# Three tiles of the first up product summed during the opening, and the second batch moved around the end of the weight conversion

## The chip, the core and the metric

The kernel runs on one core of a Trainium2 chip. The metric is device time in microseconds (us) of one execution. Five engines work side by side, each in its own order of instructions: PE (TensorE, matmuls; PEld is its weight loads), DVE (VectorE), ACT (ScalarE), POOL (GpSimd) and SP (SyncE, which here issues nearly all DMAs). [...]

## The reference

The inputs are `q`, `k`, `v` of shape 8 batches x 8 heads x 576 positions x 64, all float32, `g_norm` of 64, and the weights `w_in` (512 x 2048) and `w_out` (2048 x 512), which arrive as 64-bit floats and have to be turned into float32 on the chip.

```python
kv  = np.einsum('bhsd,bhse->bhde', k, v)
out = np.einsum('bhsd,bhde->bhse', q, kv)
rms = np.sqrt(np.mean(out * out, axis=-1, keepdims=True) + 1e-06)
x   = (out / rms * g_norm)            # then (B,H,S,D) -> (B*S, H*D): 4608 x 512
h   = x @ w_in
g   = np.maximum(h, 0.0) ** 2
y   = g @ w_out                       # 4608 x 512
```

## The kernel before

The 4608 tokens are cut into nine strips of 512 (`s` = 0 to 8). Each strip has an "up" part (times `w_in`), a squared ReLU and a "down" part (times `w_out`). From strip 1 on the products are seven block products in place of eight (`p` = 1 to 7, order `ORDER = (1, 2, 6, 5, 7, 3, 4)`), which need sums of blocks, made on DVE. Strip 0 is computed while the weights are still being converted, so its up part is the plain product: 16 tiles of `d_ff`, each four matmuls of 128x512 (`up_first`, L609), one per pair of heads. The 16 tiles use PSUM banks by the tag `"ABAC"[2 * fh + i]`: A has two buffers, B and C one each. So tile 5 needs the bank of tile 1, tile 6 that of tile 2, and so on. ACT empties a tile (ReLU L616 and square L617, twice each).

**The conversion.** 32 pieces of 512 KB come from DRAM (SP, L193) into eight `raw` buffers. For each, ACT does two instructions (L205 into a tile `w_c`, of which there are four, and L208), then DVE four (L217, L219, L223, L226). Pieces are converted in pairs; pieces 0 to 15 are `w_in`, 16 to 31 are `w_out`, and the last four pairs (`sums_out`) also take eight subtractions (L243) and four DMAs of the block sums `wt` to the DRAM tensor `w_out` (L276). `convert(n)` emits the pairs below `n`, with ACT's two instructions running one pair ahead. In the loop over the 16 up tiles the conversion is emitted ahead of the tile:

```python
if s == 0 and i < n_up:
    convert(5 + (3 * i + 2) // 4)
    ...
fn(*a)
```

**The opening.** Batch 0 is taken pair of heads by pair of heads (`p` = 0 to 3): `transposed_query` T (PE transposes L334, copied by ACT), `key_value` K (L352, copied by ACT L354, L355), `first_queries` Q (L433), `first_normalized` N (DVE, to L440), `first_features` F (PE transposes L457, copied by ACT L458 into `xT`). Between them lie the first four pieces. Their order is a list written out by hand, `slices`, of which `attend(n)` emits all up to number `n`. Every engine executes in the order in which its instructions are emitted.

**The second batch.** Its eight T and K slices are emitted after up tiles 8 to 15 (T, K, T, K, ...); T and K share two PSUM banks (tag `at`), so a slice needs the copy of the slice two before it. Its queries (L383), norms and features follow in the first six steps of strip 0's down part. Its loads (L120, L128) and those of the rest rows (L143, L151) are issued at up steps 2 and 4 and by K itself.

**Down, strips 0 and 1.** `down(s, p, i)` is one half of a block product (L573, 16 matmul rows of 128x256 per half, 32 per `p`). Its weights are `w_in`'s spare room for `p` = 1, 2, 5 of strip 0, and else a tile `w_blk` loaded from DRAM by `stream()` (L657). Strip 1 also makes the weights for the later, deeper strips: `deep_sums` (DVE, L243, four per `p`) fills a tile `w_t`, which is written to the DRAM tensor `w_deep` (L696). `w_blk` and `w_t` share four buffers. Two DMAs in flight never share one of eight completion counters, so each DMA also waits for the one eight before it.

## Time and profile before

| | us |
|---|---|
| median of 8 runs | 943.46 |
| lowest, highest | 941.71, 945.88 |
| the profiled execution | 944.16 |
| its span on the core | 942.4 |
| around the span | 1.76 |
| PE busy / DVE busy / ACT busy | 917.2 / 658.1 / 227.0 |
| first matmul of strip 0's up part | 31.0 |
| first matmul of strip 0's down part | 95.8 |
| strip 1: first up and first down matmul | 149.9, 207.8 |
| strip 2: first up matmul | 259.2 |

Times in views of the trace are us from the start of the span. A row of a timeline has start, duration, engine, line, operation, output and input, and the number of instructions merged into it; in square brackets stands the idle time in front of it, and what ended it. One fp32 matmul shows as two matmul rows, so "x8" for L609 is one tile of four matmuls.

### The profile page before, as it was taken

Reading aid. Unit: us, or ns where it says so; the run is one execution under the profiler, and the core shown is the slowest. Engines: PE = TensorE matmul, PEld = TensorE weight load, DVE = VectorE, ACT = ScalarE, POOL = GpSimd, SP = SyncE. Lnnn points to the kernel's source line nnn. Section 1 sums busy time; section 2 is a strip of 40 time slices with the busy share of each in tenths; the row PEclk is TensorE's granted clock in tenths of the full one; section 3 lists DMA queues with packets and bytes.
Section 4 is the critical chain, followed back from the end, with each engine's and each line's share of the span. In section 5 each row is a group of like instructions: output and inputs, shape, how many; then the busy total and the mean of one; then the engine's idle time right before and its main releaser. Section 6 shows DMA issues by size and latency. Waiting matters only on the chain.

```text
span 942.4 us, 17026 instructions
## 1 busy us (share of the span) xinstructions
PE 917.2 (97%) x6880; PEld 806.1 (86%) x6880; DVE 658.1 (70%) x1147; ACT 227.0 (24%) x494; POOL 1.7 (0%) x7
## 2 busy tenths in 40 slices
PE   5899999999899999999999999999999999999998
PEld 4444887888788998899989998899889988998898
DVE  4999845585436996489737975697559854983496
ACT  4797332320023102210222013200320022002200
POOL 0000000000000000000000000000000000000000
PEclk9899999999999999999999999999999999999999
DMA  9799782637875586648664874477516831681075
GB/s 276 247 280 313 261 243 107 138 109 251 286 242 138 177 299 195 148 154 290 212 155 113 312 245 126 111 282 254 165 40 236 298 102 57 224 304 65 1 260 177
DMA packets 164286, 185.94 MB, mean 197 GB/s; under 512 B 83952, under 2 KB 137712, under 8 KB 155632
## 3 DMA queue, kind: packets, MB, share of 16 engines
q1 hardware_dynamic: 163888, 184.72, 61.2%
q8 instruction: 54, 0.88, 0.4%
q10 hardware_dynamic: 320, 0.13, 0.1%
q14 instruction: 24, 0.20, 0.1%
HBM read 153.62 MB, written 31.20 MB: 196 GB/s over the span
## 4 chain that ended last, share of the span: by engine, by line
PE 90%; DMA 4%; DVE 3%; ACT 1%; issue 1%; SPq 0%; DVEq 0%; ACTq 0%
PE ps_A L573 30%; PE ps_B L758 18%; PE ps_B L573 14%; PE ps_A L758 14%; PE ps_C L573 7%; PE kv_ps L352 2%; PE x_ps L383 2%; PE ps_A L609 2%; DMA raw<-in_moe_w_out_dram 1%; DMA k_rest<-in_k_dram 1%; DMA w_blk<-w_out 1%; PE ps_B L609 1%; DVE w_c L223 1%; DMA raw<-in_moe_w_in_dram 1%; PE ps_C L609 0%
## 5 line engine op out<-in xcount | busy, mean ns | idle before, releaser
L573 PE MATMUL ps_A<-x_t,w_in 128*128 128x256 f32 x768 | 183.2, 381 | 0.0
L573 PEld LDWEIGHTS ps_A<-x_t,w_in 128*128 128x128 f32 x768 | 144.4, 190 | 20.3 <-ACT snap L583 0.3
L758 PE MATMUL ps_B<-w_blk,g_s 128*128 128x128 f32 x896 | 109.2, 275 | 0.0
L758 PEld LDWEIGHTS ps_B<-w_blk,g_s 128*128 128x128 f32 x896 | 104.6, 192 | 0.0
L758 PE MATMUL ps_B<-w_blk,gt 128*128 128x128 f32 x672 | 84.2, 275 | 0.0
L758 PE MATMUL ps_A<-w_blk,g_s 128*128 128x128 f32 x672 | 81.9, 275 | 0.0
L758 PEld LDWEIGHTS ps_B<-w_blk,gt 128*128 128x128 f32 x672 | 80.1, 192 | 0.4
L758 PEld LDWEIGHTS ps_A<-w_blk,g_s 128*128 128x128 f32 x672 | 78.4, 192 | 0.0
L632 DVE TENSOR_TENSOR gt<-ps_A,snap 128x512 f32<-128x512 f32 x32 | 22.1, 691 | 73.9 <-PE ps_A L573 73.9
L583 ACT COPY snap<-ps_A 128x512 f32<-128x512 f32 x68 | 39.8, 586 | 135.7 <-PE ps_A L573 126.9
L633 DVE SCALAR_TENSOR_TENSOR gt<-gt 128x512 f32<-128x512 f32 x96 | 66.4, 692 | 3.3
L632 DVE TENSOR_TENSOR gt<-ps_C,snap 128x512 f32<-128x512 f32 x32 | 22.1, 690 | 63.4 <-PE ps_C L573 63.4
L758 PE MATMUL ps_A<-w_blk,gt 128*128 128x128 f32 x504 | 63.1, 275 | 0.0
L573 PE MATMUL ps_A<-xT,w_in 128*128 128x256 f32 x256 | 61.3, 382 | 0.0
L573 PE MATMUL ps_C<-xT,w_in 128*128 128x256 f32 x256 | 61.1, 381 | 0.0
L573 PE MATMUL ps_B<-xT,w_in 128*128 128x256 f32 x256 | 61.0, 381 | 0.0
L573 PE MATMUL ps_B<-x_t,w_in 128*128 128x256 f32 x256 | 61.0, 381 | 0.0
L243 DVE TENSOR_TENSOR gt<-gt 128x2048 f32<-128x2048 f32 (+1 forms) x31 | 58.1, 1873 | 4.0 <-PE ps_C L573 3.8
L758 PEld LDWEIGHTS ps_A<-w_blk,gt 128*128 128x128 f32 x504 | 59.7, 192 | 0.0
L573 PEld LDWEIGHTS ps_B<-xT,w_in 128*128 128x128 f32 x256 | 48.2, 190 | 6.7
L573 PEld LDWEIGHTS ps_B<-x_t,w_in 128*128 128x128 f32 x256 | 48.2, 190 | 6.7
L573 PEld LDWEIGHTS ps_C<-xT,w_in 128*128 128x128 f32 x256 | 48.1, 190 | 6.7
(116 smaller groups left out, 1171.7 us busy)
## 6 DMA issues: line engine op xcount, KB each, us to landing
w_blk<-w_deep SPq DMA_DIRECT2D x49, 1024.0 KB, 5.2
w_blk<-w_out SPq DMA_DIRECT2D x49, 768.0 KB, 5.1
w_blk<-w_out SPq DMA_DIRECT2D x11, 1024.0 KB, 6.9
raw<-in_moe_w_in_dram SPq DMA_DIRECT2D x16, 512.0 KB, 5.6
raw<-in_moe_w_out_dram SPq DMA_DIRECT2D x16, 512.0 KB, 5.6
k<-in_k_dram SPq DMA_DIRECT2D x30, 256.0 KB, 2.9
v<-in_v_dram SPq DMA_DIRECT2D x30, 256.0 KB, 3.2
w_deep<-w_t SPq DMA_DIRECT2D x7, 1024.0 KB, 8.5
```

Of the source, the lines that this page charges most:

```text
L223: yield nc.vector.scalar_tensor_tensor(out=ci, in0=high, scalar=-(2**30), in1=ci, op0=ALU.bitwise_and, op1=ALU.bitwise_or)
L243: eng.tensor_tensor(out=out, in0=a, in1=b, op=ALU.subtract)
L352: nc.tensor.matmul(ps[ts(h, D)], lhsT=a, rhs=w, start=c == 0, stop=c == C)
L383: nc.tensor.matmul(ps[half, r, i, ts(p, D)], lhsT=q[row, half], rhs=kvd[b, p][row, row], start=True, stop=True)
L573: nc.tensor.matmul(bank[BANK[p]][:, i, :], lhsT=lhsT(k), rhs=rhs(k), start=p in (1, 5, 2) and i == 0 and k == 0, stop=k == n - 1, skip_gro ...
L583: nc.scalar.copy(snap[p], b)
L609: nc.tensor.matmul(ps, lhsT=w_in[:, kc % KH, g, kc // KH * 2 + fh, ts(i, P)], rhs=xt[0][:, :, kc, :], start=kc == 0, stop=kc == NP - 1,)
L632: nc.vector.tensor_tensor(out=o, in0=b, in1=a, op=ALU.add)
L633: nc.vector.scalar_tensor_tensor(out=o, in0=o, scalar=0.0, in1=o, op0=ALU.max, op1=ALU.mult)
L758: nc.tensor.matmul(chain[c][x][:, i, :], lhsT=a[:, f, :], rhs=w[:, f, :], start=p not in (6, 7, 3) and j in ((1, 2) if place(s, p) is LAST ...
```

## The change

1. `first_up` (U) computes part of tiles 0, 1 and 2 in the opening: as soon as a pair of heads `p` has its `xT`, one matmul for each of the three tiles adds it to the tile's bank. The twelve matmuls are the same as before; `up_first` then finds the tile done. U stands at six places in the list of slices.
2. To have banks of their own, the first queries use a tag of the `apsum` pool of the opening (`opsum`, closed at its end, and its four banks are given to the old `apsum`), and all four F use the bank C.
3. At up step 0 the ReLU of tile 0 is emitted ahead of the conversions, not behind them.
4. The second batch: its T and K are emitted after up tiles 10 to 15 and in the first two down steps, its queries from the third down step on, four slices for three steps. Its rest rows are loaded at up step 4 (were 2), its pairs of heads at 5, 7 and 9 (were 2 and 4), the third into a buffer of its own (`spare`). Batch 2's first loads and the two block sums move by one to four steps.
5. The six writes of `w_in`'s spare room to `w_out` are issued one by one after `p` = 1, 2, 5 of strip 0, not all in front of the down part.
6. In strip 1 the write of `w_t` to `w_deep` is issued right behind the sums that make it (`i == 0`), ahead of the next `stream()`, not behind it.
7. The pool `c` (snapshots and output tiles) is opened at the start, in room of its own.

```diff
-    apsum = ctx.enter_context(tc.tile_pool(name="apsum", bufs=2, space=bass.MemoryType.PSUM))
+    opening = ExitStack()
+    apsum = opening.enter_context(tc.tile_pool(name="opsum", bufs=2, space=bass.MemoryType.PSUM))
...
+        if b == 1 and p == 2:
+            h_place = spare_pool.tile([P, 3, C * P], FP32, name="more_qkv")
...
     def first_queries(p):
-        ps = fpsum.tile([P, NT, P], FP32, name="x_ps", tag="A", bufs=2)
+        ps = apsum.tile([P, NT, P], FP32, name="x_ps", tag="first")
...
-        ps = fpsum.tile([P, NT, P], FP32, name="xt_ps", tag="BC"[p % 2])
+        ps = fpsum.tile([P, NT, P], FP32, name="xt_ps", tag="C")
...
+    def first_up(p, tiles):
+        for j in tiles:
+            if p == 0:
+                first_sums[j] = fpsum.tile([P, STRIP], FP32, name=f"ps_{TAG_UP[j]}", tag=TAG_UP[j], bufs=2 if TAG_UP[j] == "A" else 1)
+            fh, i = divmod(j, 2)
+            nc.tensor.matmul(
+                first_sums[j], lhsT=w_in[:, p % KH, 0, p // KH * 2 + fh, ts(i, P)], rhs=xt[0][:, :, p, :],
+                start=p == 0, stop=p == NP - 1,
+            )
...
-    slices += [(T, (0, 3)), (K, (0, 3)), (piece, (2, 2)), (N, (2,)), (Q, (3,)), (F, (1,)), (piece, (2, 1)), (N, (3,))]
-    slices += [(act, (3,)), (F, (2,)), (piece, (2, 1)), (piece, (3, 4)), (F, (3,))]
+    slices += [(T, (0, 3)), (K, (0, 3)), (U, (0, [0])), (piece, (2, 2)), (N, (2,)), (Q, (3,)), (F, (1,)), (U, (0, [1, 2]))]
+    slices += [(piece, (2, 1)), (N, (3,)), (act, (3,)), (F, (2,)), (U, (1, [0])), (piece, (2, 1)), (piece, (3, 4)), (F, (3,))]
+    slices += [(U, (1, [1, 2])), (U, (2, [0, 1, 2])), (U, (3, [0, 1, 2]))]
...
         if i == 0:
             if s == DEEP - 1:
                 deep_sums(p, w)
+                nc.sync.dma_start(out=w_deep[B_OUT[p]], in_=deep.pop(p))
             return
         del w_blk[s, p]
         if s == 0 and p in (6, 7, 3) or s == DEEP - 1 and p not in (3, 4):
             stream()
-        if s == DEEP - 1:
-            nc.sync.dma_start(out=w_deep[B_OUT[p]], in_=deep.pop(p))
+        if s == 0 and p in (1, 2, 5):
+            for e in range(2):
+                nc.sync.dma_start(out=w_out[B_OUT[p], :, e], in_=w_first[B_OUT[p]][:, :, ts(e, P)])
...
-                convert(5 + (3 * i + 2) // 4)
-                if i in (2, 4):
+                if i > 0:
+                    convert(5 + (3 * i + 2) // 4)
+                if i in (5, 7, 9):
                     load_next()
-                if i == 2:
+                if i == 4:
                     load_q_rest(0, nc.sync)
...
             fn(*a)
+            if s == 0 and i < 1:
+                convert(5 + (3 * i + 2) // 4)
...
-            n_kv = ready[0] + 2 * NP
-            if i < n_up:
-                attend(ready[0] + max(0, (i + 1) - n_up + 2 * NP))
-            else:
-                attend(n_kv + (goal - n_kv) * min(i + 1 - n_up, 6) // 6)
+            n = i + 1 - (n_up - 6)
+            pairs, m = divmod(max(n - 2 * NP, 0), 3)
+            attend(min(ready[0] + min(max(n, 0), 2 * NP) + 4 * pairs + (0, 2, 2)[m], goal))
```

## The prediction

> **What bounds the kernel now.** First the page: PE is busy 97% of the span, so a gain can come only from PE's gaps and from matmuls at a lower clock. The view of waits, for PE alone, says where the gaps are:

> ```profile
> PE x_ps L433 <- ACT kv_all L355: 4.3, 4, 1.6
> PE xt_ps L457 <- DVE x_n L440: 3.4, 2, 2.3
> PE ps_A L573 <- DMA w_blk<-w_out: 2.1, 1, 2.1
> PE xt_ps L470 <- DVE x_n L424: 1.7, 1, 1.7
> PE kv_ps L352 <- ACT kv_all L355: 1.4, 1, 1.4
> ...
> PE ps_A L573 <- ACT snap L583: 0.7, 1, 0.7
> ...
> PE ps_B L573 <- DMA w_blk<-w_out: 0.5, 1, 0.5
> ```

> The first two lie in the opening, the fifth at the end of strip 0's up part, the snapshot in its down part, the others in strip 1 (the timeline puts the last two w_blk waits at 252 and 243 us). Nothing after that waits. Next, PE's timeline around the end of the opening:

> ```profile
> 27.14 0.66 PE L457 MATMUL xt_ps<-ident,x_n 128*128 128x128 f32 x4 [1.10 <-DVE x_n L440]
> 30.13 1.09 PE L457 MATMUL xt_ps<-ident,x_n 128*128 128x128 f32 x4 [2.33 <-DVE x_n L440]
> 31.01 5.84 PE L609 MATMUL ps_A<-xT,w_in 128*128 128x512 f32 x8
> 36.69 3.60 PE L609 MATMUL ps_B<-xT,w_in 128*128 128x512 f32 x8
> ```

> The first up tile takes 5.84 us, the next 3.60: the granted clock, read in windows of half a microsecond, is 0.50 from about 28.7 to 35.5. Last, the chain that ended last. It leaves PE at 55.7 us, runs on through raw pieces and DVE, and comes back to PE only here:

> ```profile
> 84.72 7.17 DMA raw<-in_moe_w_out_dram
> ...
> 91.98 0.67 ACT w_c L205
> ...
> 94.77 0.22 ACT kv_all L355
> 94.98 0.04 issue
> 95.03 0.80 PE kv_ps L352 x20
> 95.83 3.65 PE ps_A L573 x16
> ```

> PE has done its 16 tiles at 93.6, but the bank for the next K is freed by an ACT copy queued behind ACT's two steps on the last raw piece. The conversion, not PE, sets when the down part starts.

> **The opening.** The twelve matmuls cost 3.43 / 4 = 0.86 us each, 10.3 in all; none is new. One fits in PE's gap between K and Q of pair 3 (22.84 to 24.45), two behind the second F, one behind the third. The fourth F still waits for DVE until 30.13. It takes 0.6 at full clock, then eight matmuls follow: 30.13 + 0.6 + 8 x 0.86 = 37.6. Before, three tiles were done at 43.7. PE gains a lead of 6.1 us, of which 2.2 (5.84 - 3.60) because I expect no drop of the clock: the gap ahead of the fourth F shrinks from 2.33 to about 1.0. The queries' own banks and the single bank of the F's cost nothing: each F finds the copy of the one before done (26.9 for the third, 29.8 for the fourth), except the third, which starts 0.5 later behind two matmuls; its copy isn't due before 29.1, so that hides it.

> **Why the lead is not kept.** Tile 0's ReLU now stands ahead of pieces 6 and 7 in ACT's queue and waits for the tile's last matmul, 30.13 + 0.6 + 6 x 0.86 = 35.9. It takes 1.5 us, the two pieces 2.3, and DVE ends this pair at 42.6 where it ended at 40.9: +1.75. From there DVE goes at its own 3.75 us a pair (6.43 for the last four). Tile 1's ReLU stands behind pieces 12 and 13, whose `w_c` tiles come free as DVE finishes 8 and 9. It ran at 46.4 and will run at 48.1. Tile 5 needs that bank: it can start at 49.2 (before 50.4), while tile 4 is done at 44.3. PE sits idle for 4.9 us. What is late next is the conversion itself, and PE's lead ends as waiting.

> **The loads.** In the present order the second batch's loads stand ahead of pieces 22 to 27 on SP, and DVE waits for those pieces:

> ```profile
> 67.86 0.43 DVE L217 TENSOR_SCALAR w_c<-w_c 128x512 f32<-128x512 f32 x1 [0.38 <-ACT w_c L205]
> 71.84 0.43 DVE L217 TENSOR_SCALAR w_c<-w_c 128x512 f32<-128x512 f32 x1 [0.47 <-ACT w_c L205]
> 73.46 0.43 DVE L217 TENSOR_SCALAR w_c<-w_c 128x512 f32<-128x512 f32 x1 [1.19 <-ACT w_c L205]
> ```

> In the new order pieces 22 and 23 come ahead of all of them, 24 and 25 behind the rest rows alone; they are needed 3 to 5 us after I expect them. So these 2.04 us go, at best all (at worst none, as ACT's steps also lie behind more ReLUs); I take 2.0, and ACT, then nearly as busy as DVE, gives 0.1 back. With +1.75 the conversion ends some 0.3 earlier, the last raw piece lands at 91.5 (before 91.9), and the copy that frees K's bank ends at 94.6: **-0.4**. The third pair of batch 1 is loaded earlier, into its own buffer, and the next load still waits for a K that PE finishes at 76.5, before SP reaches it.

> **Strip 0's down part.** K of pair 3 and T and K of the pairs before it were done ahead of the wait; now T 3 and K 3 come behind it. K 2 takes the place of K 3 at the wait; so one T (0.6 + 0.15) and one K (0.8) are added to what follows: **+1.55**. The queries, norms and features only change places with halves of the products. The last sum for `p` = 5 (L600) now stands on DVE behind a query's norm: the query ends on PE at 108.7, ACT's squares 1.1, reduction and root 2.9, norm 1.3 and sum 0.7 give 114.0, and PE needs it at 114.8. It just fits. The wait for the snapshot (0.66) is now filled by transposes (0.9): **-0.66**. The six writes of w_in's room leave SP, where they blocked it for 15 us; nobody waited. The last two land at about 126, and DVE overwrites that room at 131.

> Strip 0 in sum: -0.4 + 1.55 - 0.66 = **+0.5**.

> **Strip 1's down part.** This is where I see the gain. The two waits for w_blk are 0.46 + 2.08 = 2.54 us. SP's rows:

> ```profile
> 235.92 0.32 SPq L657 DMA_DIRECT2D w_blk<-w_out  x1
> 236.33 0.38 SPq L696 DMA_DIRECT2D w_deep<-w_t  x1
> 242.54 0.32 SPq L657 DMA_DIRECT2D w_blk<-w_out  x1
> ```

> The load at 235.92 waited for the write of `w_t` issued at 227.34. The load at 242.54 waited for PE's last use of its buffer. Now each write goes out as soon as its sums are done (231.4 in place of 236.3 for `p` = 5), its buffer is free earlier, and the last load gets this buffer: it can go out at about 239, lands 7 to 9.5 us later (6.9 and 9.5 are rows of this load), and PE needs it at 249.9. The price: the load for `p` = 7 goes out 0.95 later (227.7, was 226.75) and behind a write. With the median landing of 6.9 it is there at 234.6, and PE needs it at 235.4; with the longest landing of the view of w_blk, 11.8, PE waits 4.1. I take 0.45 for this and the load after it: 2.54 - 0.45 = **-2.1**, between -2.5 and +1.6.

> **The sum.** +0.5 - 2.1 = -1.6. Against the profiled execution 944.16 - 1.6 = 942.6; that execution lies 0.7 above the median, so the forecast for the median is 943.46 - 1.6 = 941.9.

> **The rivals.** *The conversion keeps its pace* (faster). The +1.75 doesn't come, because ACT gets to pieces 6 and 7 early enough or DVE catches up. For it: DVE has small gaps elsewhere. Against it: from 37 to 67 us DVE's rows follow without a gap, so nothing can be caught up. Then -1.6 - 1.75 = -3.3: 940.1.

> *The clock* (slower). PE has a new gap of about 2 us ahead of K 2 (92.5 to 94.6), and still gaps ahead of the fourth F. If it is at half clock there, the first matmuls behind K 2 lose what the first up tile lost, 2.2. If it falls at the fourth F too, tile 0's last matmul comes at 37.4 in place of 35.9, and the conversion is 1.5 later: +3.7 together, 943.46 + 2.1 = 945.6. It decides if PE is idle for more than about half of some 3.4 us there: before, the clock fell at 28.7, with PE busy for 1.45 of the 3.4 us ahead, and held at 25.2, with 1.9. [...]

> *The write ahead of the load* (strip 1). If the load for `p` = 7 comes 2 us late, strip 1 gains nothing and the sum is +0.5: 944.0.

> *The change only moves waiting* is in the forecast already: I give the early matmuls no gain of their own.

> **How the numbers follow.** 0.2% is 1.9 us, about what a measurement of this kernel can tell from no change. Forecast 0.50, own range 940.4 to 943.5 (strip 0 between -0.5 and +1.5, strip 1 between -2.5 and -1.5): some 0.22 of it below 941.6, the rest within. The conversion keeps its pace 0.23, nearly all faster. The clock 0.16, all but 0.01 slower; the write 0.11, of which 0.08 within and 0.03 slower. Faster 0.44, same 0.38, slower 0.18. The range for 8 in 10, from the first rival's lower end (all gains whole, 939.0) to nearly the second's time: 938.8 to 945.4.

> **What would show it.** Right: the clock stays 1.00 from 28 to 37; tile 2 is done near 37.6; PE waits about 5 us for tile 1's ReLU ahead of tile 5; DVE ends pieces 6 and 7 near 42.6 and the conversion at 98 to 99; K's wait ends at 94 to 95; the two w_blk waits near 250 are gone. Wrong: a first down matmul several us ahead of 95, or half clock behind 94 us, or a new wait for w_blk at `p` = 7.

## The result, and the profile after

| | us |
|---|---|
| predicted | 941.9 (938.8 to 945.4) |
| median after, 25 runs | 941.52 (939.39 to 943.42) |
| median before, all 67 runs | 944.68 (941.05 to 949.58) |
| ratio after / before | 0.9967, interval 0.9958 to 0.9976 |

The change is worth 0.33%, 3.1 us (2.3 to 4.0). The forecast had the direction and the range, and half of the size: -1.6.

The profiled execution after took 944.17 us, with a span of 942.4, just that of before. It lies 2.65 us above the median of the runs after, so it can't be read as a whole, only stage by stage. Every profile of this study is divided at the same five points: F (the fourth F starts), D (first matmul of strip 0's down part), first up matmul of strip 1, of strip 2, and first down matmul of strip 2. The table has one profiled execution per kernel (the runs e1 to e13 are described below) and, at the right, the ratio of the timed runs to those of the kernel before.

```
                      F       D     D-F   strip 0  strip 1  strip 2   timed ratio (interval)
                                           down              up
before              30.13   95.76  65.63   54.09   109.32   54.64
after               30.64   95.06  64.42   54.33   106.27   58.18   0.9967 (0.9958-0.9976)
e1 write alone      29.87   94.14  64.27   55.02   106.31   54.65   0.9973 (0.9955-0.9992)
e2 write back       29.48   94.27  64.79   54.32   107.71   56.10   0.9986 (0.9966-1.0006)
e3 ReLU behind      30.50   96.29  65.79   56.65   106.26   55.38   0.9946 (0.9925-0.9967)
e5 no early sums    31.78   96.26  64.48   54.33   106.27   55.01   0.9958 (0.9937-0.9978)
e6 old batch        29.26   97.62  68.36   55.06   106.30   54.71   0.9977 (0.9959-0.9995)
e7 late stream      30.81   95.33  64.52   54.33   106.26   55.95   0.9979 (0.9960-0.9998)
e8 ReLU, loads      30.66   94.16  63.50   54.33   106.27   55.96   0.9921 (0.9894-0.9949)
e9 e8 and e7        28.58   90.28  61.70   54.33   106.26   55.39   0.9928 (0.9899-0.9956)
e10 e8, no early    28.85   90.27  61.42   54.33   106.27   56.41   0.9934 (0.9918-0.9950)
e11 e8, first pair  30.21   91.33  61.12   54.33   106.27   55.95   0.9930 (0.9914-0.9946)
e12 loads alone     30.76   95.36  64.60   54.33   106.27   55.04   0.9960 (0.9944-0.9976)
e13 before+w+loads  31.87  103.24  71.37   53.72   106.31   55.29   1.0017 (1.0002-1.0032)
```

F itself moves by 3 us between executions (28.6 to 31.9). At the extremes it goes with how long PE's matmuls run slower in the opening: in e9 and e10 (F at 28.6 and 28.9) the T of the fourth pair takes 0.60 us, at 19.9 and 20.4, in e5 and e13 (31.8 and 31.9) it takes 1.06, at 23.9, and the Q ahead of it 2.08 where the last Q of each takes 1.16. That hides much of what one profile could say of strip 0. The other columns repeat far better: strip 1 is 106.3 in all twelve profiles with the new place of the write. In the old batch order (before, e1, e6, e13) one T and one K less stand behind D, so D itself is later by as much for them.

The first two rows: D came 0.70 earlier, strip 1 took 3.05 less, and strip 2's up part took 3.54 more. Here is the view of waits of the kernel after, for PE:

```profile
PE ps_B L633 <- ACT gt L640: 4.8, 1, 4.8
...
PE kv_ps L358 <- DMA v<-in_v_dram: 2.3, 2, 1.8
...
PE kv_ps L358 <- ACT kv_all L361: 0.8, 1, 0.8
```

Against before, both waits for `w_blk` and the one for the snapshot are gone. The wait ahead of K has shrunk from 1.4 to 0.8. Two are new: 4.8 us for tile 1's ReLU, as forecast, and 1.8 us of a K for its `v`, which was not. The timeline of PE shows where they lie:

```profile
37.97 3.60 PE L633 MATMUL ps_C<-xT,w_in 128*128 128x512 f32 x8
41.40 3.60 PE L633 MATMUL ps_A<-xT,w_in 128*128 128x512 f32 x8
49.81 5.87 PE L633 MATMUL ps_B<-xT,w_in 128*128 128x512 f32 x8 [4.81 <-ACT gt L640]
...
94.33 0.69 PE L358 MATMUL kv_ps<-more_qkv 128*64 128x64 f32 x16 [0.81 <-ACT kv_all L361]
...
278.45 0.69 PE L358 MATMUL kv_ps<-v,k 128*64 128x64 f32 x16 [1.78 <-DMA v<-in_v_dram]
...
279.19 3.52 PE L595 MATMUL ps_A<-x_t,w_in 128*128 128x256 f32 x8
```

Tile 2 is done when tile 3 starts, at 37.97 (before 43.55): a lead of 5.6 us, or 6.1 from F. Tile 5 waits 4.81 and then takes 5.87 in place of 3.60, at half clock (0.50 granted from 47.38 to 54.21). The lead is gone twice over: 4.8 + 2.3. At 279 the same happens once more: a wait of 1.78 and then a group of 3.52 that otherwise takes 1.99 (0.50 granted from 279.49 to 282.90).

### The profile page after: what moved, and what is told of

It is laid out like the page before. It is cut to its first block, busy times and chain, and to the rows that moved or that the text cites. A ratio compares the mean times of both kernels' runs of the same rounds, so it can differ in the third digit from the quotient of the medians.

```text
span 942.4 us, 17011 instructions
## 1 busy us (share of the span) xinstructions
PE 917.9 (97%) x6880; PEld 807.3 (86%) x6880; DVE 657.8 (70%) x1147; ACT 226.7 (24%) x494; POOL 1.7 (0%) x7
## 4 chain that ended last, share of the span: by engine, by line
PE 89%; DVE 4%; ACT 3%; DMA 3%; issue 1%; SPq 0%; DVEq 0%; ACTq 0%
PE ps_A L595 29%; PE ps_B L785 18%; PE ps_B L595 15%; PE ps_A L785 14%; PE ps_C L595 7%; PE kv_ps L358 2%; PE x_ps L389 2%; DMA v<-in_v_dram 1%; DVE w_c L229 1%; ACT raw L214 1%; ACT w_c L211 1%; DMA raw<-in_moe_w_in_dram 1%; DMA k_rest<-in_k_dram 1%; DMA raw<-in_moe_w_out_dram 1%; ACT gt L641 0%
## 5 line engine op out<-in xcount | busy, mean ns | idle before, releaser
L657 DVE SCALAR_TENSOR_TENSOR gt<-gt 128x512 f32<-128x512 f32 x96 | 66.4, 692 | 3.3
L595 PEld LDWEIGHTS ps_C<-xT,w_in 128*128 128x128 f32 x256 | 48.1, 190 | 6.7
```

The lines of the kernel that those rows point to most:

```text
L595: nc.tensor.matmul(bank[BANK[p]][:, i, :], lhsT=lhsT(k), rhs=rhs(k), start=p in (1, 5, 2) and i == 0 and k == 0, stop=k == n - 1, skip_gro ...
L657: nc.vector.scalar_tensor_tensor(out=o, in0=o, scalar=0.0, in1=o, op0=ALU.max, op1=ALU.mult)
```

## The experiments

Microseconds beside a ratio are its distance from 1 times 944.7, the median before. Each ratio is to runs of the kernel before that were taken beside it: their median was 944.99 for e1 to e5, 945.22 for e6 to e9, and 943.99 for e10 to e13, which ran on another chip. A profile is of one execution. The ratios of e8 to e11 rest on 6 runs each, e12's on 7, the others on 12.

**e1: the write of `w_t` alone.** The kernel before, with part 6 and nothing else.

```diff
             if s == DEEP - 1:
                 deep_sums(p, w)
+                nc.sync.dma_start(out=w_deep[B_OUT[p]], in_=deep.pop(p))
             return
...
-        if s == DEEP - 1:
-            nc.sync.dma_start(out=w_deep[B_OUT[p]], in_=deep.pop(p))
```

> The kernel before with one edit, part 6: the write of w_t is issued right behind its sums, ahead of the next load of w_blk. Theory (the gain sits in strip 1 and comes from this edit): the two waits of strip 1's down part for w_blk (2.08 and 0.46 us) go, strip 2's first matmul comes near 256.2 (before 259.17), and the time falls by about 3.0 us, ratio 0.997, less whatever the K of strip 2's third pair then waits for its v (1.78 in the profile of the changed kernel, and up to 1.7 more for a lower clock behind it). Rival (the waits went because SP and the other transfers were moved around strip 0): both waits stay, strip 2 begins at 259, ratio 1.000.

Measured: strip 1 takes 106.31 (before 109.32), no wait for `w_blk` is left, and the ratio is 0.9973 (0.9955 to 0.9992): -2.6 us (-4.3 to -0.8). Strip 2's up part is 54.65, so nothing is given back in this execution. The theory stands, the rival falls. This one moved line is most of the whole change. SP's rows of strip 1 in the profile after show how:

```profile
226.84 0.33 SPq L715 DMA_DIRECT2D w_deep<-w_t  x1
227.27 0.38 SPq L681 DMA_DIRECT2D w_blk<-w_out  x1
230.88 0.32 SPq L715 DMA_DIRECT2D w_deep<-w_t  x1
231.65 0.32 SPq L681 DMA_DIRECT2D w_blk<-w_out  x1
237.79 0.32 SPq L715 DMA_DIRECT2D w_deep<-w_t  x1
238.21 0.37 SPq L681 DMA_DIRECT2D w_blk<-w_out  x1
```

Before, the last two loads went out at 235.92 and 242.54. Now they go out 4.3 us earlier each, as their buffers come free earlier.

**e2: the write put back.** The changed kernel with part 6 alone undone (the same diff, reversed).

> The changed kernel with part 6 alone undone: the write of w_t stands behind the load of w_blk again. Theory: the waits for w_blk near 243 and 251 come back with 2.5 to 3 us in sum, strip 1's first up matmul stays at 149.4, strip 2's comes near 258.7, and the time is that of the kernel before less about 0.5 us: ratio to it 0.9995. Rival (the other parts removed the waits): no wait for w_blk, strip 2 at 255.7, ratio 0.997.

Measured: one wait of 0.94 us at 249.32 came back, strip 1 takes 107.71, and the ratio is 0.9986 (0.9966 to 1.0006): -1.3 us. The direction is as expected, but strip 1 loses 1.44 of the 3.05 us and not all: loads and writes of this stretch are issued at nearly the same places as before (the last load at 241.24, before 242.54, both right behind PE's `p` = 7), but it landed in 7.9 us, not 9.5. The waits before depended on one late landing as well as on the order. e1 and e2 add up to -3.9 where the whole change gives -3.1; within their intervals that is the same.

**e3: the conversions ahead of tile 0's ReLU again.** The changed kernel with part 3 undone.

```diff
-                if i > 0:
-                    convert(5 + (3 * i + 2) // 4)
+                convert(5 + (3 * i + 2) // 4)
...
-            if s == 0 and i < 1:
-                convert(5 + (3 * i + 2) // 4)
```

> The changed kernel with part 3 alone undone: the conversions are again emitted ahead of tile 0's ReLU. Theory (DVE sets the end of the conversion): DVE's gaps of 1.37 and 0.71 us for pieces 6 and 7 go, the conversion ends near 96.8 (98.9 in the changed kernel), PE waits some 2 us more for tile 0's bank near 41 and about 5 us in all as before, the K ahead of the down part starts near 92.5 (94.33), strip 1 near 147.6 (149.39): 1.8 us less than the changed kernel, ratio to the kernel before 0.995. Rival (the last raw pieces set it: SP issues their loads behind writes and the second batch's loads, at 84.87): the K starts at 94 in any case, ratio 0.997.

DVE's timeline in the changed kernel has the forecast gaps for pieces 6 and 7, and no other until the conversion's end (the last row is the first sum behind it):

```profile
38.59 0.43 DVE L223 TENSOR_SCALAR w_c<-w_c 128x512 f32<-128x512 f32 x1 [1.37 <-ACT w_c L211]
39.73 0.43 DVE L223 TENSOR_SCALAR w_c<-w_c 128x512 f32<-128x512 f32 x1 [0.71 <-ACT w_c L211]
...
98.88 0.69 DVE L622 TENSOR_TENSOR g_s<-gt 128x512 f32<-128x512 f32 x1
```

In e3 these gaps are gone, and the same 2.08 us stand at the other end:

```profile
91.35 0.43 DVE L223 TENSOR_SCALAR w_c<-w_c 128x512 f32<-128x512 f32 x1 [1.16 <-ACT w_c L211]
92.69 0.43 DVE L223 TENSOR_SCALAR w_c<-w_c 128x512 f32<-128x512 f32 x1 [0.92 <-ACT w_c L211]
98.80 0.68 DVE L622 TENSOR_TENSOR g_s<-gt 128x512 f32<-128x512 f32 x1
```

ACT waited 6.8 us for raw piece 30, which landed 7.8 us after its issue at 82.8 (5.1 and 5.6 for the two pieces in the profile after). So in this execution K comes as late as the rival had it, but not for its reason: without the gaps SP issued the piece 2 us earlier (84.87 in the changed kernel), and it still landed 0.6 later. PE then waited 4.76 us at 95.02 and ran slower behind it: the first 16 rows of the down part took 6.05 us, the next 16 of the same kind 3.62. The median is another matter: 940.94, ratio 0.9946 (0.9925 to 0.9967), -5.1 us, some 2 us below the changed kernel's with the two intervals overlapping. The profiled execution (945.09) was the slowest of the twelve. How late the raw pieces land differs between executions of one code (piece 31: 7.2 us in the profile before, 6.3 in e1's).

**e5: no early sums.** The changed kernel with the opening's list of before and the conversions ahead of tile 0's ReLU.

```diff
-    slices += [(T, (0, 3)), (K, (0, 3)), (U, (0, [0])), (piece, (2, 2)), (N, (2,)), (Q, (3,)), (F, (1,)), (U, (0, [1, 2]))]
...
-    slices += [(U, (1, [1, 2])), (U, (2, [0, 1, 2])), (U, (3, [0, 1, 2]))]
+    slices += [(T, (0, 3)), (K, (0, 3)), (piece, (2, 2)), (N, (2,)), (Q, (3,)), (F, (1,)), (piece, (2, 1)), (N, (3,))]
+    slices += [(act, (3,)), (F, (2,)), (piece, (2, 1)), (piece, (3, 4)), (F, (3,))]
```

> The changed kernel without the early sums: the opening's list and the order of tile 0's ReLU are those of the kernel before, parts 4 to 7 stay. Theory (PE's lead is lost as waiting anyway): the clock drops again near 28.7 to 35.5, tile 2 is done near 44, there is no wait of 4.8 us ahead of tile 5, PE ends tile 15 near 92 to 93, DVE has neither the load stalls (2.04 us) nor the gaps of pieces 6 and 7, the K ahead of the down part starts between 92.5 and 94.3; the time is that of the changed kernel or up to 1.8 us less, ratio to the kernel before 0.995 to 0.997. Rival (the early sums carry strip 0's part of the gain): tile 15 ends later than 94.5, strip 1 begins at 150.5 or later, 1 us or more above the changed kernel, ratio 0.998 or above.

Measured: ratio 0.9958 (0.9937 to 0.9978), not told apart from the change itself. D-F is 64.48 (after: 64.42). PE ended tile 15 at 92.5 and waited 2.99 us for ACT's copy behind the raw pieces. No gain of the early sums shows here; the banks of part 2 stayed in this run.

**e12: only the load order.** In the profiles up to here, and in e6 and e7, the first of the last two raw pieces (30) was issued at 82.8 to 85.0, behind the loads of batch 1's fourth pair (768 KB). e12 is the changed kernel with that pair loaded behind them.

```diff
-            if b == 1 and p < 2:
+            if b == 1 and p == 1:
                 load_next()
...
-                if i in (5, 7, 9):
+                if i in (5, 7, 9, 12):
                     load_next()
```

> The changed kernel with one edit: the fourth pair of batch 1 is loaded behind the last two raw pieces, not ahead of them; tile 0's ReLU stays ahead of the conversions. Theory (in the changed kernel DVE's two gaps near 38, 2.08 us, and the late raw pieces are two limits of the same size, and either alone keeps the conversion's end): the pieces land at 87 to 88, DVE still ends the conversion near 98.9, the K ahead of the down part starts near 93.5 (PE's tile 15 ends there; 94.33 in the changed kernel): 0.5 to 0.8 us less than the changed kernel, ratio to the kernel before 0.996. Rival (the load order alone makes e8's gain): strip 1 begins at 147 or before, ratio 0.993.

Measured: piece 30 is at ACT at 88.58 (90.03 in the changed kernel), DVE ends the conversion at 99.00, as expected, and the K starts at 94.63 with no wait, straight behind tile 15. Ratio 0.9960 (0.9944 to 0.9976), as the changed kernel within the intervals. But ACT's copy had freed K's bank at 93.33, 0.95 earlier than in the changed kernel. It was PE that came late, as it had waited for the `q` of batch 1's first pair:

```profile
73.84 0.63 PE L340 MATMUL t_ps<-ident,q 128*128 128x128 f32 x4 [1.32 <-DMA q<-in_q_dram]
```

So with the load order alone the end of the conversion stays, but K could have started earlier.

**e8: both limits away.** e3 and e12 together.

> The changed kernel with part 3 undone (the conversions ahead of tile 0's ReLU, as in e3) and with the fourth pair of batch 1 loaded behind the last two raw pieces and not ahead of them (768 KB less in front of them on SP). Theory B: the last raw pieces land at 88 to 89.5 and not at 90 to 92, DVE waits less than 0.8 us for them in all, the conversion ends near 97, the K ahead of the down part starts near 93 (95.02 in e3, 94.33 in the changed kernel), PE's wait there shrinks from 4.8 to about 2.5, the clock stays up or loses one window: strip 1 begins at 147.5 to 149.5, ratio to the kernel before 0.993 to 0.995. Rival (the transfers of this stretch are full whatever their order): the pieces land at 90 to 92 again, K starts at 94.5 to 95, ratio as e3, 0.995, or worse where T of this pair now waits for its q near 98.

Measured: the raw pieces were issued at 80.65 and used at 86.32, DVE has no gap at all up to 96.66, and ACT's copy ahead of K ends at 90.7, 3.6 us earlier than in the changed kernel. D is at 94.16, later than that allows, since PE was stopped elsewhere: it waited 2.25 us for the `q` of batch 1's first pair (T at 71.03), and ran slower behind it: the next tile took 4.69 us, at full clock 3.60. The ratio is 0.9921 (0.9894 to 0.9949), -7.5 us (-10.0 to -4.8), clear of the changed kernel's. The ratio is as good as forecast (0.993 to 0.995) or better. The expected place of K (93) was right by luck: K waited for PE and not for the bank.

The theory of two limits side by side fits the end of the conversion on DVE (98.88 after, 98.80 in e3, 99.00 in e12, 96.66 in e8). It doesn't fit K, as the times of the last raw pieces show:

```
               DVE: last      SP: piece  piece 31  ACT's copy  K starts
               step on 26     30 issued  landed    done
before         82.79          84.06      91.89     94.98       95.03
after          82.82          84.87      91.20     94.28       94.33
e3 ReLU        80.47          82.82      91.92     94.97       95.02
e12 loads      82.95          83.01      90.24     93.33       94.63
e8 both        80.59          80.65      87.60     90.67       93.43
```

In all 14 profiles ACT's copy ends 3.05 to 3.09 us after piece 31 has landed, wherever DVE's conversion ends. And piece 30 is not issued before DVE's last step on piece 26. With the fourth pair loaded late (e8 to e13) it goes out 0.06 us behind that step in each profile, so by these times that step frees its buffer. With that pair ahead, SP issues it 1.3 to 2.6 us behind the step in the other eight. SP's rows, in the kernel after and then in e8:

```profile
82.01 0.93 SPq L126 DMA_DIRECT2D k<-in_k_dram  x1
...
84.87 1.22 SPq L199 DMA_DIRECT2D raw<-in_moe_w_out_dram  x2
...
80.65 1.13 SPq L199 DMA_DIRECT2D raw<-in_moe_w_out_dram  x2
```

So DVE's gaps and the load order are two links of one chain, and at the issue of piece 30 they add up: 2.05 us earlier than in the kernel after in e3, 1.86 in e12, 4.22 in e8. What e3's profile lost again is the landing, 8.4 us for piece 31. The timed runs of e3, e12 and e8 lie 2.0, 0.7 and 4.4 us below the changed kernel's, each within some 2 to 3 us, which can't tell adding up from more or less.

**e11: and the first pair earlier.** e8 with `load_next` at up steps 4, 7, 9, 12 and the rest rows at step 5 (were 5, 7, 9, 12 and 4).

> e8 with the first pair of batch 1 loaded at up step 4 and the rest rows at step 5 (they were loaded in the other order, the pair at step 5). In e3, e8 and e9 PE waited 0.8 to 2.3 us near 70 for this pair's q, and in e8 the clock fell there. Theory: q is there at 64, the wait goes, tile 15 ends near 90 to 91, the K ahead of the down part starts at 90 to 92 without half clock ahead of it: 1 to 3 us less than e8 where e8 had that wait, ratio to the kernel before 0.990 to 0.992. Rival (what PE gains it then waits for ACT's copy behind the last raw pieces, or pieces 20 and 21 come late behind the pair): ratio 0.992 or above, DVE waits for pieces 20 and 21 near 66.

Measured: the wait of 2.25 became one of 0.36, D is at 91.33, and D-F is 61.12, the shortest of all. The ratio is 0.9930 (0.9914 to 0.9946): by the timed runs it is the same as e8. Whether e8's wait was not in most of its runs or costs little is not shown.

**e10: e8 without the early sums** (e5 and e12 together).

> e8 without the early sums: the opening's list of the kernel before, the conversions ahead of tile 0's ReLU, the fourth pair of batch 1 behind the last raw pieces; parts 4 to 7 stay. It asks whether PE's lead of the opening is worth anything once the raw pieces land in time. Theory (yes, then PE sets the start of the down part): the last raw pieces land at 86 to 88, DVE waits little, the conversion ends near 97, but PE, some 6 us behind with half clock near 30, ends tile 15 at 92 to 93; the K starts there without waiting for ACT, strip 1 begins at 147 to 148, 1 to 3 us later than e8 would without its own wait for q (2.25 us near 69): ratio to the kernel before 0.994 to 0.995, e8 0.992. Rival (the early sums are still worth nothing): the K starts no later than in e8, ratio 0.992.

Measured: D-F 61.42, ratio 0.9934 (0.9918 to 0.9950). No different from e8, e9 and e11. The expectation was that PE's lead counts once the pieces land in time. By the profile the rival won (K at 89.54, in e8 at 93.43); the interval of the ratio holds both. PE's rows in e11 show where the lead goes even then:

```profile
37.54 3.60 PE L633 MATMUL ps_C<-xT,w_in 128*128 128x512 f32 x8
43.39 5.40 PE L633 MATMUL ps_A<-xT,w_in 128*128 128x512 f32 x8 [2.25 <-ACT gt L640]
```

Tile 4 waits 2.25 for tile 0's bank, and takes 1.8 longer at half clock (0.50 granted from 44.4 to 47.8): 4.1 of the 5.1 us that e11 leads at tile 3 (7.33 behind F; e10: 41.31, 12.46 behind F). A further 0.4 is the wait at 70. What is left is D-F of 61.12 against 61.42: 0.3 us in two profiles, which is within chance.

**e6: the old second batch.** The changed kernel with part 4 undone: loads at up steps 2 and 4, T and K from up tile 8 on, the third pair in the old buffers.

> The changed kernel with part 4 alone undone: the second batch's loads, T, K and queries stand where they stood in the kernel before. Theory A (DVE's pace sets the end of the conversion): DVE's waits for pieces 20 to 23 come back (about 2.0 us) on top of its gaps for pieces 6 and 7, the conversion ends near 101, the K ahead of the down part starts near 96.5, one T and one K less stand behind it (-1.3): strip 1 begins near 150, 0.6 to 1 us later than in the changed kernel, ratio to the kernel before 0.9975. Theory B (the landing of the last two raw pieces sets it, near 90 to 92 in every run so far): the conversion ends near 99 and the K starts near 94 to 95 all the same, strip 1 begins near 148.5, ratio 0.996.

Measured: DVE's waits for pieces are back (1.22 and 0.81 at 73 and 74, 0.48 at 94), the conversion ends at 100.38, K starts at 96.61, D-F is 68.36, and the ratio 0.9977 (0.9959 to 0.9995). Theory A. With the old order of the loads the conversion ends 1.5 us later, 2.9 counted from F, and behind PE's wait of 2.43 the first 16 rows of the down part took 5.05 us, the next 16 of the same kind 3.72.

**e13: the kernel before, with the write and the load order.**

```diff
-            if b == 1 and p < 2:
+            if b == 1 and p == 0:
...
-                if i in (2, 4):
+                if i in (2, 4, 12):
```

> The kernel before with two edits: the write of w_t ahead of the next load of w_blk (as e1), and the fourth pair of batch 1 loaded behind the last two raw pieces. No early sums, the old second batch. Theory: strip 1 gains its 3.0 us, the last raw pieces land near 87 and not at 92, so the K ahead of the down part starts when PE's tile 15 ends (93.6 by the profile of the kernel before, where it starts at 95.03): 1.0 to 1.4 us more, ratio to the kernel before 0.995 to 0.996. Rival (only part 4's order frees the stretch, and DVE's waits for pieces 20 to 23 keep the conversion late): ratio 0.997, as e1.

Measured: ratio 1.0017 (1.0002 to 1.0032), +1.6 us; D at 103.24. Neither theory saw it:

```profile
95.70 1.08 PE L334 MATMUL t_ps<-ident,q 128*128 128x128 f32 x4 [5.56 <-DMA q<-in_q_dram]
...
96.79 5.79 PE L609 MATMUL ps_C<-xT,w_in 128*128 128x512 f32 x8
```

In the old order the T of that fourth pair stands ahead of tile 15. Its `q`, loaded late, stops PE for 5.56 us, and tile 15 runs slower behind it: 5.79 us, at full clock 3.60. So part 4, which moves this T behind D, is what makes room for the better load order. I had priced the load's delay and not asked which matmul needs it.

**e7: strip 2's loads spread.** The changed kernel, with the four loads of `w_blk` for strip 2 at its up steps 9, 12, 15 and 18.

```diff
                     sums_x(s + 1)
-                    stream(4)
...
+                if s == DEEP and i in (9, 12, 15, 18):
+                    stream()
```

> The changed kernel with one edit: the four loads of w_blk for strip 2 are issued one by one after its up steps 9, 12, 15 and 18, not all at the end of strip 1. They are first needed at strip 2's down part, near 314 in the profile. Theory (the wait of strip 2's third K for its v, 1.78 us, and the half clock behind it, 1.7, come from the write of x_d: it takes 9.8 us among these four loads, and SP's loads of k and v stand behind it): the write lands in some 3 us, k and v are issued near 265 and not 273, the wait goes, strip 2's down part begins near 310.3 in place of 313.84; in the timed runs, some of which had less of this wait, 1 to 2 us less than the changed kernel, ratio to the kernel before 0.995. Rival (it was one late landing in one execution, or the loads of w_blk come late now): no difference in the median, ratio 0.997, or a new wait for w_blk near 310.

Measured: the write of `x_d` and its reads are 2.05 us apart (9.86 in the changed kernel), `v` is issued at 266.1, and the K's wait is gone. But PE now waits 1.04 and 0.33 for DVE at 310 and 314: DVE had stopped 2.97 us for a later write of `x_d`, which now meets the loads. Strip 2 takes 55.95, the ratio is 0.9979 (0.9960 to 0.9998): the rival. The stall moved.

**e9: e8 and e7 together.**

> e8 and e7 together: part 3 undone, the fourth pair of batch 1 loaded behind the last raw pieces, the four loads of w_blk for strip 2 spread over its up steps. Theory: the gains add, 1.5 to 2 us of e8 and 1 to 2 of e7 below the changed kernel, ratio to the kernel before 0.992 to 0.994. Rival: what strip 0 gains is given back at strip 2 or in PE's lower clock, ratio 0.995 or above.

Measured: ratio 0.9928 (0.9899 to 0.9956), as e8. e7's edit adds nothing here either. D at 90.28 with F at 28.58.

e8 to e11 all beat both kernels; they take 0.66 to 0.79% less than the kernel before. The simplest of them is e10: parts 2 and 4 to 7, the list of slices of before, and one load moved by one step.

## Why the prediction was right or wrong

*The number.* In part luck. The forecast took 1.6 us off the median of the first eight runs before, 943.46, which lies 1.2 below that of all 67 (944.68). So 941.9 comes within 0.4 of the measured 941.52, though the change is worth about twice the 1.6.

*The opening.* Right within 0.6 us in each number, with F itself 0.5 later in this execution: the clock stayed at 1.00 from 28 to 37, tile 2 was done at 37.97 (37.6), DVE ended pieces 6 and 7 at 43.15 (42.6), tile 5 started at 49.81 (49.2) after 4.81 us (4.9). Also right that the lead is not kept: e5 and e10, without it, are not told apart from the runs with it. (Tile 4's 44.3 should be 37.6 + 2 x 3.43 = 44.5.)

*The loads.* DVE's waits for pieces 20 to 23 (2.0) went, and e6 brought them back. The conversion ended at 98.88, in the range of 98 to 99, but no earlier than before (98.86; 0.3 earlier was forecast, and from F it is 0.5). The wait of K ended 0.70 earlier, against 0.4. That is luck: SP issued piece 31 at 85.61, 0.9 later than before, and it landed in 5.6 us in place of 7.2. What I had wrong is the reason: "the conversion, not PE, sets when the down part starts" is too wide. K follows the landing of the last raw piece, 3.1 us behind it, and not DVE's end. I put the landing down as following DVE (91.5), as if the 768 KB ahead of the pieces on SP were free. The rival *the conversion keeps its pace* looked for the gain at pieces 6 and 7; e3's profile shows none, as the pieces landed late there; its timed runs say some 2 us, with overlapping intervals, and e8 says what the two edits are worth together.

*Strip 0.* Forecast +0.5 in sum, profile -0.46 (strip 1 begins at 149.39, before 149.85). The added T and K cost 0.54 + 0.73 = 1.27, not 1.55 (I added a row's duration where the next row's start is the measure). The snapshot's wait gave back 0.74 (0.66), the wait of K 0.70, and the first transposition 0.22, as its `x_n` was ready. (The terms given for the last sum of `p` = 5 add up to 114.7 and not 114.0; it ended at 113.59, and PE did not wait.) But one code (before and e1) has D-F of 65.63 and 64.27 in two executions, so 1 us of strip 0 can't be told from chance by two profiles. The timed runs of e2 (all but the write) say -1.3 (-3.2 to +0.6).

*Strip 1.* The mechanism was right and the term too small: -2.1 forecast, -3.05 measured. The 0.45 for a late load at `p` = 7 didn't come: it was issued at 227.27 as forecast (227.7), the three last loads landed in 7.3 to 9.3 us, and PE needed this one 7.67 later and did not wait: a margin of 0.4 us at most. The rival *the write ahead of the load* missed by that. And two waits of 2.54 us cost 3.01: from 207.81 to 259.17 the part took 51.36, without them 48.35. So each of these waits costs about a quarter of a microsecond more than its idle time.

*Strip 2.* Not in the prediction at all: I read "nothing after that waits" off the profile of before, and held it for the new one. Strip 2 now begins 3.5 us earlier, but SP's reads of `x_d`, with `k` and `v` behind them, only 3.1 earlier, as the write of `x_d` takes 9.8 us among four loads (before: 9.4). `v` for the third K went out 3.07 before PE could use it (before: 3.44), and landed in 4.7 (before: 3.1; the median of these loads is 3.2). The margin before was some 0.3 us or less. In this execution that cost 3.54 us; the other profiles with the new write have 54.65 to 56.41 in this part. What it costs in the timed runs, no run shows by itself.

*The clock.* The rival had it ahead of K, where the gap was 0.81 and nothing fell. It did fall at tile 5 (0.50 from 47.4 to 54.2), where it cost 2.3 us of PE's time. I take it to have cost nothing of the whole, since K then waited for ACT all the same. By the rival's own sign (PE idle for more than half of 3.4 us) the forecast wait of 4.9 us had to bring this drop, and it was not priced there. It fell again at 279 (0.50), where it cost 1.5 of 3.5 us. The bound of 939.0 in the range is not worked out in the prediction; its own terms give 938.7 (-0.5, -1.75 and -2.5).

## What to carry to other kernels

Ask of a lead on the busiest engine which buffer or bank stops it next: here 5 to 6 us of PE's work done early became 0.3 us in the profiles of e11 and e10, since the banks of the tiles came free at another engine's pace. Follow a wait past its last link: K waited for ACT, ACT for a landing, the landing for the place of its load in SP's order, and that load for a buffer that DVE frees. An edit at one link can be hidden by a late landing (e3's profile) or by another engine that comes late (e12's), so time the pair of edits as well (e8). A transfer issued a step later is priced by the instruction that needs it, in the order that this kernel has: the same move took 3 us off D-F in one order (e5 to e10) and cost 4 us of the whole in the other (e1 to e13).

## What the runs showed of the hardware

```profile
43.97:47.38 3.41, 1.03 (x3) 0.19 (x1) 3.41 (x8) 2.05 (x4) 0.00 (x0) 1.00 0.86 264
47.38:50.79 3.41, 0.98 (x1) 0.50 (x2) 3.41 (x8) 3.35 (x9) 0.00 (x0) 0.50 0.97 327
276.07:279.49 3.42, 1.64 (x24) 1.18 (x23) 0.00 (x0) 0.78 (x2) 0.00 (x0) 1.00 0.90 171
```

All three were followed by half clock (0.50). In e8 the wait for tile 0's bank fell differently on the grid, and the step behind it kept full clock:

```profile
40.17:43.58 3.41, 1.42 (x4) 0.35 (x2) 3.41 (x9) 3.12 (x7) 0.00 (x0) 1.00 0.87 262
43.58:46.99 3.41, 3.15 (x8) 1.44 (x8) 3.41 (x8) 3.35 (x8) 0.00 (x0) 1.00 0.95 333
```

In e5 the wait of 2.99 us ahead of K was shared by two steps, and the clock held behind both:

```profile
90.42:93.83 3.41, 2.12 (x5) 0.58 (x4) 1.98 (x7) 2.44 (x5) 0.00 (x0) 1.00 1.13 345
93.83:97.24 3.41, 1.71 (x25) 1.54 (x26) 3.41 (x8) 3.25 (x11) 0.00 (x0) 1.00 1.06 318
```

In the 14 profiles, from 20 us on, a drop began behind steps with 0.00 (e3, from 90.80) to 1.64 us of PE busy, one of them with 1.42 (before, from 25.28). The clock held, among others, behind 1.42 (e8), 1.59 (e1, from 23.27), 1.71 (e5), 1.77 (after, from 156.61), 1.78 and 1.80 (before, from 250.56 and 21.87). So every drop seen began behind a step that was less than about half busy, and between 1.4 and 1.7 the clock fell behind some steps and held behind others. The length of the wait alone doesn't tell: 1.78 us brought the drop in the kernel after, 2.08 (before, at 252) and 2.99 (e5) did not.

**Landings spread where the transfers were full.** The last raw pieces took 5.1 to 5.6 us from issue to landing in the profile after and 7.8 to 8.4 in e3, at a DMA share of 1.08 and 1.00 between 80 and 92 us (the mean busy share of the 16 DMA engines, by their packets' times). Before and e1, with one code here, have 7.2 and 6.3 for piece 31. A gain of 1 us in such a stretch needs timed runs: the profiled executions of the changed kernel, e3, e8 and e13 were each slower than every other run of theirs.
